# Score products in visits of three chunks, with a three-deep PSUM ring shared with the gate sums

## The chip, the cores and the metric

The kernel runs on one core of one Trainium2 chip. The metric is the device time of an execution in microseconds, given as the median of several executions. The span in a profile is mostly about 1.8 us shorter than the time of the same execution, since it starts and ends with the first and last recorded instruction.

## The reference

Softmax attention over 8 batches and 12 heads, then a gated feed-forward layer on the 3584 tokens:

```python
# q, k, v: (8, 12, 448, 64); w_gate, w_val: (768, 1536); w_out: (1536, 768)
scores = np.matmul(q, k.transpose(0, 1, 3, 2)) / np.sqrt(64)
attn = np.exp(scores - scores.max(-1, keepdims=True))
attn = attn / (attn.sum(-1, keepdims=True) + 1e-09)
x = np.matmul(attn, v).transpose(0, 2, 1, 3).reshape(3584, 768)
g = x @ w_gate
out = (g * (1 / (1 + np.exp(-g))) * (x @ w_val)) @ w_out
```

## The kernel before

Two heads make a pair, so there are 48 pairs, six to a batch. Scores are computed transposed, in four chunks of 112 key rows per pair. The contraction over 64 head dimensions uses half the array's rows, so the two heads of a pair lie in the two halves: the *64-row form*. The weighted sums and the row sums have outputs of 32 rows and use a quarter of the columns for each of four products: the *32-column form*, or quarter form. The feed-forward products use the whole array (*full form*), or are written in the quarter form where `tiled` is set, with four times as many instructions for the same work.

TensorE works in an order fixed by the program. It comes to the scores in *visits*: two chunks, then other work (a weighted sum, a row sum, gate, value and output groups), then two chunks. ScalarE turns scores into exponentials.

```python
ps_s = ctx.enter_context(tc.tile_pool(name="ps_s", bufs=2, space=PSUM))  # scores, 2 banks each
ps_a = ctx.enter_context(tc.tile_pool(name="ps_a", bufs=1, space=PSUM))  # weighted sums
ps_f = ctx.enter_context(tc.tile_pool(name="ps_f", bufs=3, space=PSUM))  # all the rest
# ...
def qk_half(pr, half, between=None):
    # ...
    for c in (2 * half, 2 * half + 1):
        s = ps_s.tile([128, 2, 512], FP32, tag="s")
        for hx in range(2):
            nc.tensor.matmul(s[:, hx, 0:S], lhsT=..., rhs=..., start=True, stop=True)
        nc.scalar.activation(E[pr][:, c], s[0:P, :, 0:S], AF.Exp, scale=sm_scale)
        # ...
def mm(dst, lhsT, rhs, start, stop):
    if not tiled[0]:
        nc.tensor.matmul(dst, lhsT=lhsT, rhs=rhs, start=start, stop=stop)
        return
    for j in range(4):
        nc.tensor.matmul(dst[ts(j, 32), :], lhsT=lhsT[:, ts(j, 32)], rhs=rhs, start=start, stop=stop)

def ffn1_steps(kk, c0, n, hts):
    for fb in range(NFB):
        gp = ps_f.tile([128, 512], FP32, tag="f")
        # six mm into gp (gate); tanh on ScalarE -> sg; yield
        vp = ps_f.tile([128, 512], FP32, tag="f")
        # six mm into vp (value); two products on VectorE -> hts; yield
```

The softmax here doesn't subtract the row's maximum and nothing guards it: scores larger than these inputs give would overflow.

## Time and profile before

| | before |
|---|---|
| time, median of 3 runs | 463.16 us (462.67 to 463.72) |
| span of the profiled execution | 460.2 us |
| TensorE busy | 452.3 us, 98% |
| ScalarE, VectorE busy | 53%, 51% |
| first score of pair 6 (the mixed stage starts) | 28.64 us |
| end of the last matmul | 456.60 us |

TensorE is the bound, and its busy share cannot show what the change is after, since a change of the array's form counts as busy time. It is read from start-to-start times in the timeline of TensorE, and from the list of waits. There "PEld" (the weight load) waiting on "issue" is a stall with no releaser. The lines themselves stand in the prediction below.

### The profile page before, as it was taken

The numbers are of one execution on the slowest core, as the hardware profiler recorded it, in microseconds if no ns is written. First come the engines' busy times: TensorE is split into PE (matmuls) and PEld (weight loads), VectorE is DVE, ScalarE is ACT, GpSimd is POOL, SyncE is SP. The second block draws the span as 40 slices with busy tenths as digits, with TensorE's granted clock in tenths as the row PEclk, the third lists the DMA queues.
The fourth block names the chain that finished last, engine by engine and source line by source line (L and its number), as shares of the span: only waits on it lengthen the run. The fifth ranks groups of instructions, "written<-read, shape, count | busy, mean of one in ns | idle before, by whom it ended". The sixth has DMA issues, their size and how long they took to land.

```text
span 460.2 us, 14133 instructions
## 1 busy us (share of the span) xinstructions
PE 452.3 (98%) x6367; PEld 227.8 (49%) x6367; DVE 236.8 (51%) x371; ACT 243.0 (53%) x353; POOL 104.2 (23%) x164
## 2 busy tenths in 40 slices
PE   8899999999999999999999999999999999999996
PEld 3344444444455555444455555544445556554454
DVE  2765663666764554564654554636555546334310
ACT  7986666656664555454646555455555562222222
POOL 8455606334150132303123040210200000000000
PEclk9999999999999999999999999999999999999999
DMA  9999999995793484662758393903603111100123
GB/s 133 195 200 201 192 180 183 223 154 80 90 113 57 78 126 49 114 102 31 118 58 119 67 131 74 142 6 76 98 10 56 37 37 36 36 11 25 36 68 103
DMA packets 82045, 44.23 MB, mean 96 GB/s; under 512 B 36673, under 2 KB 78529, under 8 KB 81985
## 3 DMA queue, kind: packets, MB, share of 16 engines
q0 software_dynamic: 42368, 23.37, 39.2%
q1 hardware_dynamic: 39520, 19.92, 23.8%
q8 instruction: 49, 0.80, 0.7%
q14 instruction: 12, 0.09, 0.1%
q10 hardware_dynamic: 96, 0.05, 0.0%
HBM read 47.19 MB, written 11.01 MB: 126 GB/s over the span
## 4 chain that ended last, share of the span: by engine, by line
PE 95%; ACT 3%; DMA 1%; DVE 0%; issue 0%; SPq 0%; ACTq 0%
PE gp L264 15%; PE op L261 14%; PE vp L264 13%; PE vp L261 11%; PE op L264 10%; PE s L196 10%; PE gp L261 9%; PE acc L212 9%; PE acc L234 4%; ACT E L203 2%; DMA rk<-in_k_dram 1%; PE tp L184 1%; PE wp L103 0%; PE tp L167 0%; DVE qkT L175 0%
## 5 line engine op out<-in xcount | busy, mean ns | idle before, releaser
L203 ACT ACTIVATE E<-s 112x896 f16<-112x896 f32 x192 | 164.6, 917 | 24.3 <-PE s L196 24.1
L280 ACT ACTIVATE sg<-gp 128x384 f32<-128x384 f32 (+1 forms) x96 | 52.3, 545 | 85.4 <-PE gp L264 54.7
L292 DVE SCALAR_TENSOR_TENSOR t<-sg,gp 128x384 f32<-128x384 f32 (+1 forms) x96 | 58.5, 610 | 64.3 <-ACT sg L280 64.2
L325 ACT ACTIVATE osb<-op 128x384 f32<-128x384 f32 (+1 forms) x57 | 27.7, 486 | 100.5 <-PE op L261 56.3
L264 PE MATMUL gp<-X,wg 128*32 128x512 f16 (+1 forms) x1416 | 78.1, 355 | 0.0
L249 DVE RECIPROCAL R<-ssb 128x112 f32<-128x112 f32 x92 | 73.1, 827 | 0.7
L295 DVE SCALAR_TENSOR_TENSOR hts<-t,vp 128x384 f16<-128x384 f32 (+1 forms) x96 | 59.6, 621 | 23.3 <-PE vp L264 7.9
L261 PE MATMUL op<-wo,hts 128*128 128x384 f16 (+1 forms) x408 | 68.6, 322 | 0.0
L264 PE MATMUL vp<-X,wv 128*32 128x512 f16 (+1 forms) x1224 | 66.9, 353 | 0.0
L226 DVE TENSOR_TENSOR X<-acc,R 128x448 f16<-128x448 f32 x48 | 29.7, 624 | 64.9 <-PE acc L212 63.1
L261 PE MATMUL vp<-X,wv 128*128 128x384 f16 (+1 forms) x270 | 58.4, 352 | 0.0
L196 PE MATMUL s<-qkT 64*128 64x448 f16 x384 | 54.8, 355 | 2.5 <-ACT E L203 2.2
L261 PEld LDWEIGHTS <-hts 128*128 128x128 f16 x408 | 38.9, 98 | 28.2 <-issue 3.0
L264 PEld LDWEIGHTS <-wg 128*32 128x32 f16 x1416 | 37.8, 97 | 29.6
L264 PE MATMUL op<-wo,hts 128*32 128x384 f16 x1104 | 48.9, 326 | 0.0
L261 PE MATMUL gp<-X,wg 128*128 128x384 f16 (+1 forms) x222 | 47.4, 350 | 0.0
L264 PEld LDWEIGHTS <-wv 128*32 128x32 f16 x1224 | 32.7, 97 | 25.5
L212 PE MATMUL acc<-E,vt 112*32 112x448 f16 x768 | 45.2, 355 | 0.0
L126 POOL DMA_DIRECT2D vt<-in_v_dram x16 | 12.3, 772 | 142.7 <-PE acc L212 141.7
L261 PEld LDWEIGHTS <-wv 128*128 128x128 f16 x270 | 25.3, 98 | 26.9 <-issue 4.8
L264 PEld LDWEIGHTS <-hts 128*32 128x32 f16 x1104 | 29.5, 97 | 16.3
L154 POOL COPY qk<-q 112x512 f16<-112x512 f16 x37 | 22.9, 620 | 63.9 <-DMA qkT<-qk 46.4
(38 smaller groups left out, 201.2 us busy)
## 6 DMA issues: line engine op xcount, KB each, us to landing
vt<-in_v_dram POOLq DMA_DIRECT2D x16, 336.0 KB, 5.2
q<-in_q_dram POOLq DMA_DIRECT2D x22, 224.0 KB, 5.9
k<-in_k_dram POOLq DMA_DIRECT2D x22, 224.0 KB, 6.7
out_dram<-osb SPq DMA_DIRECT2D x7, 336.0 KB, 3.1
wg<-in_moe_w_gate_dram POOLq DMA_DIRECT2D x8, 288.0 KB, 11.1
wv<-in_moe_w_val_dram POOLq DMA_DIRECT2D x8, 288.0 KB, 11.4
wo<-in_moe_w_out_dram POOLq DMA_DIRECT2D x2, 1152.0 KB, 21.6
out_dram<-osb SPq DMA_DIRECT2D x8, 288.0 KB, 2.9
```

Of the source, the lines that this page charges most:

```text
L154: nc.gpsimd.tensor_copy(dst, src)
L196: nc.tensor.matmul(s[:, hx, 0:S], lhsT=t[ts(hx, 64)].rearrange("p c q -> p (c q)")[:, c * P : c * P + 128], rhs=t[ts(hx, 64), NC:, :].rear ...
L203: nc.scalar.activation(E[pr][:, c], s[0:P, :, 0:S], AF.Exp, scale=sm_scale)
L212: nc.tensor.matmul(acc[ts(j, 32), 0:S], lhsT=v16[g][:, 2 * r + j % 2, c, :].rearrange("p (d t) -> p t d", t=2)[:, t], rhs=E[p0 + j // 2][: ...
L226: nc.vector.tensor_tensor(X[kk][:, hp + t, ts(bb, S)], acc[:, 0:S], R[p0][:], ALU.mult)
L249: lambda i=i: nc.vector.reciprocal(rt[:, ts(i, P)], ssb[:, ts(i, P)]) for i in range(4)
L261: nc.tensor.matmul(dst, lhsT=lhsT, rhs=rhs, start=start, stop=stop)
L264: nc.tensor.matmul(dst[ts(j, 32), :], lhsT=lhsT[:, ts(j, 32)], rhs=rhs, start=start, stop=stop)
L280: nc.scalar.activation(sg[:, 0:n], gp[:, 0:n], AF.Tanh, scale=0.5)
L292: nc.vector.scalar_tensor_tensor(t1[:, 0:n], sg[:, 0:n], 1.0, gp[:, 0:n], ALU.add, ALU.mult)
L295: nc.vector.scalar_tensor_tensor(hts[:, fb, 0:n], t1[:, 0:n], 0.5 * HS, vp[:, 0:n], ALU.mult, ALU.mult)
L325: nc.scalar.activation(osb[:, ds(m0, w)], op[:, 0:w], AF.Copy, scale=1.0 / HS)
```

## The change

The change makes the visits longer and so fewer: from pair 20 on, three chunks per visit in place of two. For this the score tiles become a ring of three (six of the eight PSUM banks), which the gate sums share. Value sums, weighted sums, row sums and outputs are left with two banks. The order of all the work is planned anew to fit.

```diff
+WIDE = 20
 ...
-    ps_s = ctx.enter_context(tc.tile_pool(name="ps_s", bufs=2, space=PSUM))
-    ps_a = ctx.enter_context(tc.tile_pool(name="ps_a", bufs=1, space=PSUM))
-    ps_f = ctx.enter_context(tc.tile_pool(name="ps_f", bufs=3, space=PSUM))
+    ps_s = ctx.enter_context(tc.tile_pool(name="ps_s", bufs=3, space=PSUM))
+    ps_f = ctx.enter_context(tc.tile_pool(name="ps_f", bufs=2, space=PSUM))
 ... (the first transposes take ps_s tiles, pv() takes ps_f tiles)
-            gp = ps_f.tile([128, 512], FP32, tag="f")
+            gp = ps_s.tile([128, 2, 512], FP32, tag="s", name="gp")[:, 0]
 ... (the loop over pairs with its backlog of groups is replaced)
+        while g < last or queue:
+            n = 2 if g < WIDE * NC else 3
+            todo = []
+            while queue and queue[0][0] <= g and len(todo) < 2:
+                todo.append(queue.pop(0))
+            plan.append(([divmod(x, NC) for x in range(g, min(g + n, last))], todo))
+            g += n
 ...
+        for x, (chunks, todo) in enumerate(plan):
 ...
+            for pr, c in chunks:
+                qk(pr, c)
 ... (one product, then gate-value pairs, the second product, output groups)
```

More of the change, by code (lines that the diff above doesn't have):

```diff
@@ L178, in turn @@
         def turn():
-            tp = ps_f.tile([128, 2 * NC, 128], FP16, tag="f", name="tp")
+            if pr < FIRST + 2:
+                tp = ps_s.tile([128, 2 * NC, 256], FP16, tag="s", name="tp")
+            else:
+                tp = ps_f.tile([128, 2 * NC, 128], FP16, tag="f", name="tp")
             for t in range(2):
@@ L187, in prep, with qk, qk_half, pv @@
         return turn if pr else turn0
-    def qk_half(pr, half, between=None):
-        if half == 0:
+    def qk(pr, c):
+        if c == 0:
             E[pr] = ep.tile([P, NC, 2, S], FP16, tag="E", name="E")
         t = qkT[pr]
-        for c in (2 * half, 2 * half + 1):
-            s = ps_s.tile([128, 2, 512], FP32, tag="s")
-            for hx in range(2):
-                nc.tensor.matmul(
-                    s[:, hx, 0:S],
-                    lhsT=t[ts(hx, 64)].rearrange("p c q -> p (c q)")[:, c * P : c * P + 128],
-                    rhs=t[ts(hx, 64), NC:, :].rearrange("p c q -> p (c q)"),
-                    start=True,
-                    stop=True,
-                )
-            nc.scalar.activation(E[pr][:, c], s[0:P, :, 0:S], AF.Exp, scale=sm_scale)
+        s = ps_s.tile([128, 2, 512], FP32, tag="s")
+        for hx in range(2):
+            nc.tensor.matmul(
+                s[:, hx, 0:S],
+                lhsT=t[ts(hx, 64)].rearrange("p c q -> p (c q)")[:, c * P : c * P + 128],
+                rhs=t[ts(hx, 64), NC:, :].rearrange("p c q -> p (c q)"),
+                start=True,
+                stop=True,
+            )
+        nc.scalar.activation(E[pr][:, c], s[0:P, :, 0:S], AF.Exp, scale=sm_scale)
+    def qk_half(pr, half, between=None):
+        for c in (2 * half, 2 * half + 1):
+            qk(pr, c)
             if between and c % 2 == 0:
                 between()
-    def pv(p0, t, pool=None):
-        acc = (pool or ps_a).tile([128, 512], FP32, tag="f" if pool else "acc", name="acc")
+    def pv(p0, t):
+        acc = ps_f.tile([128, 512], FP32, tag="f", name="acc")
         for c in range(NC):
@@ L228, in scaled, with sums @@
         )
-    def sums(p0):
-        acc = ps_f.tile([128, 512], FP32, tag="f")
+    def sums(p0, wide=False):
+        if wide:
+            acc = ps_s.tile([128, 2, 512], FP32, tag="s", name="acc")[:, 0]
+        else:
+            acc = ps_f.tile([128, 512], FP32, tag="f", name="acc")
         for c in range(NC):
@@ L385 @@
         deferred = []
-        backlog = []
-        state = {"left": 0.0}
         ffn2_wait = []
@@ L393, in pop_deferred, with add_block @@
                     deferred.pop(0)()
-        def add_block(i):
+        fvq = []
+        oq = []
+        count = {}
+        def add_block(i, visits):
             f1, f2, n = block(i)
-            t1, t2 = NCB * n / 2400.0, NFB * OH / 2400.0
-            a = [(f1, t1)] * (2 * NFB)
-            pend = list(ffn2_wait)
+            oq.extend(ffn2_wait)
             ffn2_wait.clear()
-            seq = []
-            m = len(pend)
-            done = 0
-            for x in range(len(a)):
-                seq.append(a[x])
-                want = (x + 1) * m // len(a)
-                while done < want:
-                    seq.append(pend[done])
-                    done += 1
-            seq += pend[done:]
-            own = [(f2, t2)] * (2 * (n // 128))
-            if i == 0:
-                seq += own
-            else:
-                ffn2_wait.extend(own)
-            backlog.extend(seq)
-            state["left"] += sum(t for _, t in seq)
@@ L419, in ffn_run @@
-        def ffn_run(budget):
-            while backlog and budget > 0:
-                gen, t = backlog.pop(0)
-                next(gen)
-                budget -= t
-                state["left"] -= t
-                pop_deferred(1 if t < 1.5 else 2)
-            return budget
-        carry = 0.0
-        DELAY = 2
-        END = NPAIR + 2
-        add_at = {FIRST: 0}
-        for i in range(1, B - 1):
-            add_at[NHP * (i + 1) + DELAY] = i
-        for pr in range(END):
-            slots = 2 * (min([x for x in add_at if x > pr] + [END + 0.5]) - pr)
+            fvq.extend([(f1, NCB * n / 2400.0)] * NFB)
@@ new lines, in add_block, with run_fv, run_o @@
+            own = [(f2, NFB * OH / 2400.0)] * (2 * (n // 128))
+            (oq if i == 0 else ffn2_wait).extend(own)
+            count.update(visits=visits, fv=NFB, o=len(oq), at=0, more=NFB - visits)
+        def run_fv():
+            gen, t = fvq.pop(0)
+            for _ in range(2):
+                next(gen)
+                pop_deferred()
+            return 2 * t
+        def run_o():
+            gen, t = oq.pop(0)
+            next(gen)
+            pop_deferred(2)
+            return t
@@ L436, with run_budget, left, share @@
+        def run_budget(budget):
+            while (fvq or oq) and budget > 0:
+                budget -= run_fv() if fvq else run_o()
+            return budget
+        def left():
+            return sum(2 * t for _, t in fvq) + sum(t for _, t in oq)
+        def share(total, at, n):
+            return (at + 1) * total // n - at * total // n
+        for pr in range(FIRST):
             odd = pr % 2 == 1
             turn2 = None
-            if pr == FIRST:
-                recip_act(pr - 2, sums(pr - 2))
-                load_table("exp_and_others")
-                halves = [pv(pr - 2, 0), pv(pr - 2, 1, ps_f)]
@@ L442 @@
-            if pr < NPAIR:
-                qk_half(pr, 0, prep(2) if pr == 1 else None)
+            qk_half(pr, 0, prep(2) if pr == 1 else None)
             if pr == 0:
@@ L447 @@
                 dummy(1)
-            if pr + 3 < NPAIR and pr + 3 >= NPE:
-                prep(pr + 3)
-            if not odd and 14 <= pr + LA < NPAIR:
-                load_qk16(pr + LA)
-            if pr + 2 < NPAIR:
-                if 0 < pr < NPE - 2:
-                    turn2 = prep(pr + 2)
-                if (pr + 2) % GP == GP - 1 and 4 <= (pr + 2) // GP + 1 < NGRP:
-                    load_v((pr + 2) // GP + 1)
-            if pr == FIRST:
-                for t in range(2):
-                    scaled(pr - 2, t, halves[t])
-                add_block(0)
-                ffn_run(2.5)
-            elif not odd and pr >= 2:
+            if pr > 0:
+                turn2 = prep(pr + 2)
+            if (pr + 2) % GP == GP - 1 and 4 <= (pr + 2) // GP + 1 < NGRP:
+                load_v((pr + 2) // GP + 1)
+            if pr in (2, 4):
                 deferred.extend(recips(pr - 2, sums(pr - 2)))
-                if pr < FIRST:
-                    pop_deferred(1)
+                pop_deferred(1)
             elif pr in (3, 5):
-                halves.append(pv(pr - 3, 1, ps_f))
+                halves.append(pv(pr - 3, 1))
                 pop_deferred(4)
@@ L470 @@
                     scaled(pr - 3, t, halves[t])
-            work = odd and pr > FIRST + 1
-            if work:
-                pop_deferred(4)
-                scaled(pr - 3, 0, pv(pr - 3, 0))
-            if pr in add_at and pr != FIRST:
-                add_block(add_at[pr])
             for w in wq.pop(pr, []):
                 emit(w)
-            tiled[0] = pr >= TILED
-            if pr != FIRST:
-                carry = ffn_run(state["left"] / slots + carry)
-            else:
-                slots -= 1
-            tiled[0] = False
-            if pr < NPAIR:
-                early = 1 <= pr < FIRST
-                qk_half(pr, 1, turn2 if early else None)
+            qk_half(pr, 1, turn2)
             if pr == 0:
                 dummy(2)
-            if turn2 and not early:
-                turn2()
             if pr in (2, 4):
@@ L494 @@
                 halves = [pv(pr - 2, 0)]
-            if work:
-                scaled(pr - 3, 1, pv(pr - 3, 1))
-            tiled[0] = pr >= TILED and work
-            carry = ffn_run(state["left"] / max(1, slots - 1) + carry)
+        p4 = FIRST - 2
+        recip_act(p4, sums(p4, True))
+        load_table("exp_and_others")
+        halves = [pv(p4, t) for t in range(2)]
+        queue = []
+        for p0 in range(FIRST, NPAIR, 2):
+            for kind, m in (("sums", 8), (0, 11), (1, 14)):
+                queue.append((NC * p0 + m, kind, p0))
@@ new lines @@
+        plan = []
+        g = FIRST * NC
+        last = NPAIR * NC
+        while g < last or queue:
[5 more added lines that the diff above has]
+            g += n
+        adds = {0: 0}
+        for x, (_, todo) in enumerate(plan):
+            for _, kind, p0 in todo:
+                if kind == 1 and p0 % NHP == NHP - 2 and p0 // NHP < B - 1:
+                    adds[x] = p0 // NHP
@@ new lines, in product @@
+        def product(kind, p0):
+            if kind == "sums":
+                pop_deferred(99)
+                deferred.extend(recips(p0, sums(p0)))
+            else:
+                pop_deferred(99)
+                scaled(p0, kind, pv(p0, kind))
+        carry = 0.0
+        for x, (chunks, todo) in enumerate(plan):
+            wide = not chunks or len(chunks) != 2
+            for pr, c in chunks:
+                qk(pr, c)
+            end = min([y for y in adds if y > x] + [len(plan) + 1])
+            if x == 0:
+                for t in range(2):
+                    scaled(p4, t, halves[t])
+                add_block(0, end)
+            turn2 = None
+            entered = [pr for pr, c in chunks if c == 0]
+            for pr in entered:
+                if NPE <= pr + 3 < NPAIR:
+                    prep(pr + 3)
+                if pr % 2 == 0 and 14 <= pr + LA < NPAIR:
+                    load_qk16(pr + LA)
+                if (pr + 2) % GP == GP - 1 and 4 <= (pr + 2) // GP + 1 < NGRP:
+                    load_v((pr + 2) // GP + 1)
+            for pr, c in chunks:
+                if c == 2 and pr < NPE - 2:
+                    prep(pr + 2)()
+            if todo:
+                product(*todo[0][1:])
+            if x in adds and x > 0:
+                add_block(adds[x], end - x)
+            for pr in entered:
+                for w in wq.pop(pr, []):
+                    emit(w)
+            tiled[0] = bool(todo) and (not chunks or chunks[0][0] >= TILED)
+            if adds[max(y for y in adds if y <= x)] < 2:
+                for item in todo[1:]:
+                    product(*item[1:])
+                carry = run_budget(left() / (end - x) + carry)
+            else:
+                at, n = count["at"], count["visits"]
+                no = share(count["o"], at, n)
+                nf = 1
+                if no and count["more"] > 0:
+                    o_left = sum(1 for y in range(at, n) if share(count["o"], y, n))
+                    extra = -(-count["more"] // o_left)
+                    nf += extra
+                    count["more"] -= extra
+                count["at"] += 1
+                for y in range(nf):
+                    if fvq:
+                        run_fv()
+                for item in todo[1:]:
+                    product(*item[1:])
+                for _ in range(no):
+                    run_o()
@@ L499 @@
             tiled[0] = False
-        ffn_run(1e9)
+        run_budget(1e9)
         pop_deferred(99)
-        add_block(B - 1)
-        ffn_run(1e9)
-        backlog.extend(ffn2_wait)
-        ffn_run(1e9)
+        add_block(B - 1, 1)
+        run_budget(1e9)
+        oq.extend(ffn2_wait)
+        run_budget(1e9)
 _INS = ['q', 'k', 'v', 'moe_w_gate', 'moe_w_val', 'moe_w_out']
```

## The prediction

> **What bounds the kernel now.** I read the page first: engine shares, the slices, the chain that ended last. Then the list of waits, and then the timeline of TensorE in single visits of the steady stage, with ScalarE beside it.
>
> ```profile
> PE 452.3 (98%) x6367; PEld 227.8 (49%) x6367; DVE 236.8 (51%) x371; ACT 243.0 (53%) x353; POOL 104.2 (23%) x164
> PE 95%; ACT 3%; DMA 1%; DVE 0%; issue 0%; SPq 0%; ACTq 0%
> ```
>
> TensorE is busy in 98% of the span and carries 95% of the chain that ended last; no other engine is above 53%. The 3% of ScalarE lie in the first 27 us, where only exponentials and scores exist. So only what TensorE itself does, or a wait put in front of it, can move the end. A busy share hides the cost that this change is after, though. It shows in the list of waits and in start-to-start times:
>
> ```profile
> PEld L196 <- issue: 35.2, 96, 0.7
> PEld L212 <- issue: 15.6, 44, 0.4
> PEld L261 <- issue: 11.8, 32, 0.4
> PEld L234 <- issue: 8.9, 25, 0.7
> PE s L196 <- ACT E L203: 2.2, 5, 0.4
> ```
>
> The weight loads of the scores (L196) stand still 96 times, once per visit to the scores, with no releaser: nothing is late, the array is being changed over. The weights cannot be loaded ahead there. What these stalls cost the matmuls is less than their 0.37 us each, because earlier matmuls still run. That is read from the starts (columns: start, duration, engine, line, operation):
>
> ```profile
> 253.68 1.15 PE L264 MATMUL gp<-X,wg 128*32 128x384 f16 x24
> 254.76 0.55 PE L196 MATMUL s<-qkT 64*128 64x448 f16 x4
> 255.24 0.94 PE L234 MATMUL acc<-E,ones 112*32 112x448 f16 x16
> 256.00 2.12 PE L264 MATMUL op<-wo,hts 128*32 128x384 f16 x48
> 257.96 1.15 PE L264 MATMUL vp<-X,wv 128*32 128x384 f16 x24
> 259.04 0.55 PE L196 MATMUL s<-qkT 64*128 64x448 f16 x4
> 259.52 1.15 PE L261 MATMUL gp<-X,wg 128*128 128x384 f16 x6
> 260.51 1.14 PE L261 MATMUL vp<-X,wv 128*128 128x384 f16 x6
> ```
>
> A gate or value group of 384 columns takes 0.98 us to the next start where another full-height group follows (median over the span), and 1.08 where scores follow (253.68 to 254.76, 257.96 to 259.04); with 512 columns 1.30 and 1.40. So entering the scores costs **0.10 us**. The four score matmuls take 0.48 us to the next start; in the early stage visits of two matmuls take 0.29. The second chunk therefore adds 0.19, and leaving the scores costs 0.29 - 0.19 = **0.10 us**. Between 128-column and 32-column form there is another 0.10 (0.87 against 0.77 for a weighted sum that full-width groups follow). In steady running both forms cost the same, 0.98 us for 6 full or 24 quarter matmuls, so writing more of the groups in the quarter form is neutral.
>
> **What the Trainium skill says.** The page "TensorEngine Tiling (Array Packing)", section "Key Properties", says that changing the tiling mode drains TensorE, while changing the tile does not. The trace agrees: 0.10 us at each change between 64-row, 32-column and full form, none inside one form. It gives no figure; the 0.10 is the trace's. The page "TensorE: Matmul & The Clock Gate", section "Back-to-back issue gap", has N/2.4 + 2.5 ns for a warm matmul: 162.5 ns for 384 columns, 0.975 us for six, and the trace's 0.98 agrees, so no slack is left inside a group. The page "PSUM — Partial Sum Buffer", section "PSUM bank collisions raise a hardware error", asks that an engine's access to a bank be ordered against the others' by semaphores: a ring slot is only reusable after its reader is done. The trace shows that wait five times, scores waiting on the exponential.
>
> **The change part by part.** From the instruction order of both kernels I counted stretches of one array form.
>
> *Switches.* Pairs 20 to 47 have 28 x 4 = 112 chunks: 56 visits of two before, 37 of three and one of a single chunk after, so 18 visits fewer. Entering scores falls from 99 to 81 times and leaving them likewise; changes between 32-column and full form fall from 12 to 10. All changes: 217 before, 179 after, 38 fewer, by 0.10 us = **-3.8 us**. A visit of three should take 0.48 + 0.19 = 0.67 us.
>
> *Columns streamed.* Unchanged; 288 full matmuls become four times as many quarters (864 more instructions), neutral by the above: 0.
>
> *Scores' ring and the exponential.* After a wide visit comes a 4-column product (0.77 us), then a gate group. In a ring of three, the visit's scores take all three slots and the gate group takes the slot of the first chunk, which must have been exponentiated. It wants to start 0.67 + 0.77 = 1.44 us after the visit's first score. When is that slot free? Columns again start and duration:
>
> ```profile
> 250.59 0.49 ACT L325 ACTIVATE osb<-op 128x384 f32<-128x384 f32 x1 [2.43 <-PE op L264]
> 250.98 1.72 ACT L203 ACTIVATE E<-s 112x896 f16<-112x896 f32 x2
> 252.93 0.49 ACT L280 ACTIVATE sg<-gp 128x384 f32<-128x384 f32 x1 [0.23 <-PE gp L264]
> ```
>
> The scores of this visit started at 250.47, right after an output group. ScalarE first copies that output out (0.12 after the first score), then starts the exponential at 0.51; with its mean of 0.917 us it ends at 1.43, and in the early stage a waiting score matmul started 0.05 us after the exponential's end. So the slot is free at 1.48 against 1.44 wanted: 0.02 to 0.04 us late. The new order has 31 wide visits directly after an output group: about **+0.9 us**. Visits after other work start their exponential at 0.40 and are in time (1.36).
>
> *Block starts.* The new order puts the first gate group of a block straight after the last weighted sum that fills its input; before, two pairs lay between. The scaling on VectorE ended 1.67 us after that sum's start (0.995 to begin, 0.624, 0.05); the sixth matmul step of a 384-column group wants it at 0.77 + 5 x 0.163 = 1.58, of a 512-column group at 1.85. Three narrow blocks lose about 0.09: **+0.25 us**.
>
> *Two banks for the rest.* Value sums, weighted sums, row sums and outputs now alternate in two banks. By the durations of the rows, in a visit with one gate-value pair the exponentials end 3.15 us in, tanh 3.64, the two VectorE products 4.8; the value bank is wanted again only in the next visit, after 6.1. That holds with two pairs as well. One place fails: where a block of 384 columns starts and a row sum is drawn into the same visit, all four reciprocals (0.75 each) stand before the next scaling, which ends 9.15 us in, while the second value group wants that bank at 8.8, and the output group after it waits again: about **+0.6 us**, once.
>
> *First six pairs.* Here ScalarE bounds; it was idle about 0.75 us between its first and last exponential there. The third score buffer should take away some, and the transposes, which now share the ring, give part of it back: **-0.3 us**.
>
> Sum: -3.8 + 0.9 + 0.25 + 0.6 - 0.3 = -2.35, so 463.16 - 2.35 = **460.8 us**.
>
> **The rivals.** First, that the switches are all there is: the waits of 0.02 to 0.09 us vanish, since in the profile before no TensorE wait exists between 29 and 381 us. Then 463.16 - 4.1 = 459.1. Second, that the ring becomes the bound: a margin of -0.04 us is no margin, and each further 0.1 us on the exponential (three in a row keep ScalarE and its queue behind for 3.15 us of a visit of 5.5 to 8.7) costs 31 x 0.1 = 3.1 us; with 0.15 the time is 465. For it: gate groups wait on an engine that serves in order. Against: ScalarE is only about half busy in this stage (108 of 200 us), and the order seems cut to fit. Third, that the gate sums in the ring delay the next visit's third score: its slot is free after tanh and the first product, by 4.3 us for one pair and about 7 for two, while it is wanted past 5.8 and 7.8; I expect no wait. Fourth, that a switch saved gives less than 0.10, since the first matmul after a switch is a little longer anyway; at 0.09 it is 0.4 us less.
>
> **Range and chances.** The gain cannot exceed about 4.8 us (all switches and all the early idle time), 458.4. Downward the unknown is the ring: 0.1 us more per visit ends near 463.9. I give 458.6 to 463.2. Two per cent are 9.3 us: no term reaches that for the better, and for the worse it would take a wait of 0.4 us in each wide visit. Faster 0.01, within 2% 0.97, slower 0.02.
>
> **What would show it right or wrong.** Right: scores' weight loads stalling on issue some 78 times in place of 96; six score matmuls in 0.67 us to the next start; 0.98 to 1.08 us groups as before; a short wait of the gate group on the exponential in most wide visits, together about 1 us; TensorE otherwise without waits after 29 us. Wrong: waits of the gate, value or output groups summing above 3 us, a third score that waits on VectorE, a visit of three that takes longer than 0.7 us, or an early stage that ends more than 1 us off its 28.6.

## The result and the profile after

The changed kernel takes **460.93 us** (median of 4 runs, 459.70 to 462.18). The kernel before takes 463.24 in the same rounds. The ratio is **0.9949**, 95% interval 0.9926 to 0.9972. The predicted 460.8 us is met.

The engine shares, the chain that ended last, and the instruction queue, from the page of the changed kernel:

```profile
PE 449.9 (98%) x7231; PEld 244.6 (53%) x7231; DVE 239.2 (52%) x371; ACT 240.3 (52%) x353; POOL 104.0 (23%) x164
...
q8 instruction: 56, 0.92, 0.9%
...
PE 93%; DVE 3%; ACT 2%; DMA 1%; issue 0%; DVEq 0%; ACTq 0%
```

TensorE still bounds the kernel, with 2.4 us less busy time. It has 864 more matmuls (7231 against 6367), since more groups are in the quarter form. The queue that fetches instructions moved 56 packets, 0.92 MB, where it had moved 49 and 0.80 MB. I gave that line no thought before the run, and it matters below.

The list of waits of the changed kernel (engine, line, what it waited for; us in total, times, longest):

```profile
PEld L198 <- issue: 28.9, 80, 0.8
PEld L218 <- issue: 15.3, 43, 0.4
PEld L243 <- issue: 7.4, 21, 0.4
...
PE s L198 <- ACT E L205: 1.5, 4, 0.4
```

L198 is now the scores' matmul. Its weight loads stall 80 times where it was 96: the visits are fewer, and 80 is near the predicted 78. TensorE's matmuls have no listed wait after 29 us. One wide visit of the changed kernel, TensorE and ScalarE from the timeline (start, duration, engine, line, operation):

```profile
251.25 0.74 PE L198 MATMUL s<-qkT 64*128 64x448 f16 x6
251.37 0.49 ACT L334 ACTIVATE osb<-op 128x384 f32<-128x384 f32 x1 [2.43 <-PE op L273]
251.75 2.52 ACT L205 ACTIVATE E<-s 112x896 f16<-112x896 f32 x3
251.93 0.94 PE L218 MATMUL acc<-E,vt 112*32 112x448 f16 x16
...
252.72 1.16 PE L273 MATMUL gp<-X,wg 128*32 128x384 f16 x24
...
253.69 1.16 PE L273 MATMUL vp<-X,wv 128*32 128x384 f16 x24
```

Six score matmuls take 0.68 us to the next start here (251.25 to 251.93), 0.67 over the median of the 37 wide visits. The weighted sum takes 0.79 to the gate group (251.93 to 252.72), where 0.77 would be without a wait. The profile does not list a loss of 0.02 us; only start-to-start times show it. Before the exponentials (251.75) ScalarE copies out the output group (251.37), as the prediction had it. With the mean of 0.92 us the first exponential ends at 252.67, and the gate group starts at 252.72.

Three other places cost time, all where a block of tokens ends or starts:

```profile
240.71 0.95 PE L243 MATMUL acc<-E,ones 112*32 112x448 f16 x16
241.76 2.13 PE L273 MATMUL op<-wo,hts 128*32 128x384 f16 x48
...
345.61 1.23 PE L273 MATMUL gp<-X,wg 128*32 128x384 f16 x24
346.66 1.16 PE L273 MATMUL vp<-X,wv 128*32 128x384 f16 x24
...
351.90 1.15 PE L273 MATMUL gp<-X,wg 128*32 128x384 f16 x24
353.14 1.16 PE L273 MATMUL vp<-X,wv 128*32 128x384 f16 x24
354.26 2.13 PE L273 MATMUL op<-wo,hts 128*32 128x384 f16 x48
```

A gate group followed by a value group of the same form takes 0.98. At 345.61 it takes 1.05, since its sixth step waits for the freshly scaled input (0.07 lost). At 351.90 it takes 1.24: the value bank is late by 0.26, and the output group after it by 0.14 more (353.14 to 354.26 is 1.12). At 240.71 a row sum takes 1.05 in place of 0.77: the output group behind it is 0.28 late. It starts at 241.76, and VectorE's product that it needs ends at 241.70 (start 241.15, duration 0.55).

From the first score of pair 6 to the end of the last matmul the kernel before takes 427.96 us (28.64 to 456.60) and the changed one 425.86 (28.44 to 454.30): 2.10 less. This stretch, called **the mixed stage** below, leaves the start out, which varies from execution to execution.

### The profile page after: what moved, and what is told of

It is laid out like the page before. It is cut to its first block, busy times and chain, and to the rows that moved or that the text cites. A ratio compares the mean times of both kernels' runs of the same rounds, so it can differ in the third digit from the quotient of the medians.

```text
span 457.9 us, 15867 instructions
## 1 busy us (share of the span) xinstructions
PE 449.9 (98%) x7231; PEld 244.6 (53%) x7231; DVE 239.2 (52%) x371; ACT 240.3 (52%) x353; POOL 104.0 (23%) x164
## 4 chain that ended last, share of the span: by engine, by line
PE 93%; DVE 3%; ACT 2%; DMA 1%; issue 0%; DVEq 0%; ACTq 0%
PE gp L273 16%; PE vp L273 16%; PE op L273 15%; PE op L270 9%; PE s L198 9%; PE acc L218 8%; PE gp L270 8%; PE vp L270 7%; PE acc L243 4%; ACT E L205 2%; DVE R L258 1%; DMA rq<-in_q_dram 1%; PE tp L187 1%; DVE X L232 0%; DVE ssb L255 0%
## 5 line engine op out<-in xcount | busy, mean ns | idle before, releaser
L273 PE MATMUL gp<-X,wg 128*32 128x384 f16 (+1 forms) x1608 | 87.9, 352 | 0.0
L273 PE MATMUL vp<-X,wv 128*32 128x384 f16 (+1 forms) x1608 | 87.8, 351 | 0.1
L273 PE MATMUL op<-wo,hts 128*32 128x384 f16 x1680 | 74.7, 326 | 0.1
L273 PEld LDWEIGHTS <-wv 128*32 128x32 f16 x1608 | 46.5, 97 | 29.2 <-issue 0.3
L273 PEld LDWEIGHTS <-hts 128*32 128x32 f16 x1680 | 49.2, 97 | 20.8 <-issue 0.6
L198 PE MATMUL s<-qkT 64*128 64x448 f16 x384 | 51.4, 353 | 2.4 <-ACT E L205 1.5
L270 PE MATMUL op<-wo,hts 128*128 128x384 f16 (+1 forms) x264 | 42.2, 319 | 0.0
L270 PE MATMUL gp<-X,wg 128*128 128x512 f16 (+1 forms) x174 | 38.3, 356 | 0.0
L270 PE MATMUL vp<-X,wv 128*128 128x512 f16 (+1 forms) x174 | 38.1, 355 | 0.0
L270 PEld LDWEIGHTS <-hts 128*128 128x128 f16 x264 | 25.1, 98 | 17.0 <-issue 1.9
L255 DVE COPY ssb<-acc 128x448 f32<-128x448 f32 x23 | 14.4, 624 | 35.2 <-PE acc L243 35.2
```

The source lines that it names most:

```text
L198: nc.tensor.matmul(s[:, hx, 0:S], lhsT=t[ts(hx, 64)].rearrange("p c q -> p (c q)")[:, c * P : c * P + 128], rhs=t[ts(hx, 64), NC:, :].rear ...
```

## The experiments

All were correct unless said otherwise. "Changes" are changes of the array's form, counted from the instruction order: 217 before, 179 in the changed kernel. The kernel before took 463.50, 463.34, 463.35 and 463.23 us in the rounds of the four chips.

### e0_again: the changed kernel unedited

> The changed kernel once more, unedited, for its spread and to stand beside the next three on one chip. All theories: 460.9 us, within 459.7 to 462.2 as its first four runs; a gate group that follows a product in a wide visit starts 0.79 us after that product (0.77 where nothing waits).

Measured: 461.51 us (460.11 to 463.24), ratio 0.9967 (0.9943 to 0.9990). The spread of 3 us is wider than that of the kernel before (462.1 to 464.43 in 11 runs of those rounds, in two clusters of spans near 460.4 and 461.7). Its profile, of a slow one among its executions, shows two causes. First, the start: the warm-up matmul of the changed kernel's first profile, and then of this one:

```profile
6.38 0.39 PE L103 MATMUL wp<-warm 128*128 128x512 f16 x1
```

```profile
6.83 0.61 PE L103 MATMUL wp<-warm 128*128 128x512 f16 x1
```

The same instruction takes 0.61 us in place of 0.39. TensorE ran slower here until about 10 us, and pair 6 started at 29.91 in place of 28.44: 1.5 us lost before the change has any part in it. The Trainium skill, page "TensorE: Matmul & The Clock Gate", section "Part 1: The HAM clock gate", says that the array starts at half clock and that the window which decides on the full clock runs freely, so that the same kernel has more or fewer slow matmuls from run to run. The traces agree: their record of the full clock begins at 4.71 us in the first profile and at 10.16 in this one. Second, in the middle of an output group:

```profile
178.56 0.68 PE L273 MATMUL op<-wo,hts 128*32 128x384 f16 x12
180.42 1.65 PE L273 MATMUL op<-wo,hts 128*32 128x384 f16 x36 [1.19 <-issue]
```

After 12 of 48 matmuls TensorE stands for 1.19 us, on "issue", with every operand long there. A value group at 288 us lost 0.41 in the same way. By start-to-start times 1.37 and 0.59 us are lost in the two, and 0.1 in a third place (252.5) without a listed wait; with the late start this is the whole difference of the spans (461.5 against 457.9). The trace's instruction fetches come in packets of 16 KB; one that started at 175.29 took 3.68 us where 0.97 is typical. It landed at 178.97, and TensorE went on 1.46 us later. So a **late instruction fetch** was the suspect. No fetch was held up on purpose, but a count over all traces, told below under what was right and wrong, bears it out.

### e1_two: visits of two to the end, with the new rings and the new planner

```diff
-WIDE = 20
+WIDE = 48
```

> Visits of two chunks to the end (WIDE = 48), all else as changed: the ring of three, two banks for the rest, the new order. Changes of array form rise from 179 to 215. My theory (each change costs 0.10 us, and that is the gain): +3.6 us, less about 0.6 us because in visits of two the gate group gets a slot whose reader is long done, less up to 0.7 us of block-start waits: 463.2 to 463.9 us, no better than the kernel before. Rival (the third score buffer and the new order make the gain, not the visits): stays at 460.9.

215 changes. Measured: 462.25 us (461.95 to 463.39), ratio 0.9986. In the profiles the mixed stage is 428.33 against 425.86, **2.47 us longer**, inside what I expected for the step from two to three chunks (3.6 less 0.6 less up to 0.7). It is also no shorter than that of the kernel before (427.96): the third buffer and the new order alone gain nothing, so the rival falls. The time itself is below the expected 463.2. The medians differ by only 0.7 (against e0_again) to 1.3 (against the first four runs), and the intervals of e1_two (0.9968 to 1.0004) and e0_again overlap, so the times alone do not decide. The profile of this kernel has no stall on issue within a group, and its runs spread 1.4 us, while those of the changed kernel spread 2.5 and 3.1.

### e7_tinyfull and e8_tinyhalf: the price of one change of form

In each wide visit, a matmul of 8 columns stands before the second and the third chunk (74 in all). In e7 it is in full form, which adds two changes of form each, 148 together. In e8 it is in the scores' own 64-row form and adds none. The chunk that follows overwrites its result.

```diff
+        if tiny:   # e8: warm[0:64, ...] in both operands
+            nc.tensor.matmul(s[:, 0, 0:8], lhsT=warm[:, 0:128], rhs=warm[:, 0:8], start=True, stop=True)
```

> The cost of a change of array form by itself: in each of the 37 wide visits a tiny matmul of 8 columns in full form (into the bank that the following scores overwrite; results stay right) is put before the second and before the third chunk, so 74 tiny matmuls and 148 changes of form more. My theory (0.10 us at each change): 14.8 us and at most 2 us for the tiny ones themselves, 475 to 478 us; a wide visit takes about 0.67 + 0.4 + a little = 1.1 us to the next start. Rival (a change costs less where it is not between long groups, or the saving lies in fewer instructions): under 470 us.

> The same 74 tiny matmuls of 8 columns in the 64-row form of the scores themselves: as many instructions, no change of form. My theory: 461 to 463 us, a wide visit about 0.7 us. Rival (the instructions cost it): as slow as with the full-form ones.

Measured: 474.56 us (474.55 to 475.88), ratio 1.0250, for e7, and 462.47 (460.89 to 463.48), 0.9979, for e8. The time of e7 is just under the expected 475. From its start to the next start a wide visit takes 1.108 us in e7, 0.718 in e8 and 0.671 in the changed kernel (medians of 37). The four changes of a visit thus cost 0.39 us, **0.097 us each**; over the 37 visits 14.4 us. The mixed stages, 440.61 and 427.63, agree: from that of e8 one issue stall is to be taken off, 1.08 by start-to-start times, which leaves 14.1 us between them. The small matmuls of e8 add 1.7 us to the visits, but the gate groups then no longer wait for the exponential (0.77 us after the product, not 0.79), so the mixed stage without the stall is only 0.7 longer than the changed kernel's. The lists of waits of e7, then e8:

```profile
PEld L200 <- issue: 28.8, 80, 0.7
PEld L198 <- issue: 14.8, 74, 0.2
```

```profile
PEld L200 <- issue: 29.0, 80, 0.8
```

The tiny loads (L198) stall 74 times in e7 and not at all in e8; the scores (L200) as before. Ordering alone, or the number of instructions, does not do it; the form does.

### e17_half: 64-column halves in place of 32-column quarters

```diff
-        for j in range(4):   # ts(j, 32)
+        for j in range(2):   # ts(j, 64)
```

> The groups in quarter form (four column tiles of 32) written in half form instead (two of 64 columns); all else as changed. 7231 matmuls become 4783, as many columns streamed. If a product of 32-column tiles followed by 64-column tiles counts as a change of form: some 50 changes more, 5 us more, about 466, a product to gate group at 0.87 to 0.89 us. If it does not, and late instruction fetches are what spreads the times of the changed kernel: no wait on issue inside a group, a spread of 1.4 us or less (the slow and fast start alone), and 460.0 to 460.5 us.

The same work with 4783 matmuls in place of 7231. Measured: 465.48 us (465.13 to 466.31), ratio 1.0052. The hope for a faster kernel fell. The list of waits has a new line, and the timeline shows what it costs:

```profile
PEld L273 <- issue: 19.1, 52, 0.4
```

```profile
255.92 0.94 PE L218 MATMUL acc<-E,vt 112*32 112x448 f16 x16
256.79 1.17 PE L273 MATMUL gp<-X,wg 128*64 128x384 f16 x12
```

From a 32-column product to a 64-column group it takes 0.87 us, not 0.77 to 0.79: going from 32 to 64 columns is itself a change of form. The mixed stage is 431.0, 5.14 more than 425.86, and 52 times 0.10 is 5.2. The Trainium skill, page "TensorEngine Tiling (Array Packing)", section "Available Configurations", lists 128x64 and 128x32 as separate configurations; together with the drain on a change of mode, that is what this run shows. I had missed it. On the other side, this kernel's profile has no stall on issue within a group, and its six runs lie within 1.2 us, which fits the late fetches.

### e13_tiled6: the quarter form from the start of the mixed stage

```diff
-TILED = 14
+TILED = 6
```

> Quarter form for the groups that follow a product from pair 6 on instead of from pair 14 (TILED = 6): changes of form fall from 179 to 170, 360 matmuls more. My prediction's step (the quarter form is neutral): 0.9 us less, 460.0 to 460.6. New theory (the quarter form quadruples the instructions that TensorE has to fetch, and where transfers are dense a late fetch stops it for about 1 us in some executions): as many or more waits on issue of a group in its middle, a wider spread of the times, and no gain: 461 to 463.

170 changes. Measured: 460.73 us (460.26 to 462.36, 6 runs), ratio 0.9949, just above the expected 460.6. The mixed stage is 425.36. One stall on issue of 0.27 at 193 us is in it (0.44 by start-to-start times), so without it 424.9: 0.96 less than 425.86, and 9 changes by 0.10 are 0.9. So the quarter form is neutral in steady running, as predicted. It also speaks against my idea that fetches come late where transfers are dense: the first 83 us are the densest of the kernel, the quarter form was put there, and no group stalled there.

### e9_late: copying an output group out after the next visit's first exponential

```diff
+                if hold[0]:
+                    yield 0.0
                 nc.scalar.activation(osb[:, ds(m0, w)], op[:, 0:w], AF.Copy, scale=1.0 / HS)
```

Where the next visit has three chunks, the copy is held back and issued after the first chunk's exponential.

> In the wide stage the copy of an output group out of its bank is put on ScalarE's queue behind the first exponential of the next visit instead of ahead of it. My theory (the gate group waits 0.02 us in each of some 31 visits because that copy delays the exponential from 0.40 to 0.51): product to gate group falls from 0.79 to 0.77 us and the time by 0.6 us, to about 460.3. Rival (the 0.02 us is the changeover or the weight load, not the exponential): 0.79 and 460.9 stay.

Measured: 460.38 us (459.33 to 462.1), ratio 0.9934 (0.9914 to 0.9953). From the product to the gate group it takes 0.77 where it was 0.79, so the wait on the ring is gone. In the changed kernel 31 gate groups were 0.022 to 0.033 late, 0.79 us in all; here none is. Also, the scores that follow an output group came 2.070 us after its start in the changed kernel and come 2.056 after it here, as in the kernel before (0.36 in all); why they were late was not looked into. The mixed stage of its profile is 426.64, with two stalls on issue (1.12 and 0.2 by start-to-start times). Without them it would be 425.3, 0.5 below 425.86: a longer wait (a value group on VectorE's scaling, 0.56 where it was 0.27) and lesser ones take back part of the 1.15. Its interval overlaps that of e0_again, so by times alone the gain is unclear; the start-to-start times show it.

### e14_first: e9_late, with the visit's second product straight after the first

```diff
+            if len(chunks) == 3:
+                for item in todo[1:]:
+                    product(*item[1:])
+                todo = todo[:1]
```

> Two waits taken out of the changed kernel: the copy-out behind the first exponential of the next visit (as in the earlier run that was faster), and, where a visit has two products, both straight after the scores, so that the reciprocals start about 2 us earlier and the first gate group of a block comes 0.77 us later. My theory: product to gate group 0.77 us; the waits at the block starts (0.07 to 0.09 us three times), of an output group on the products of VectorE (0.29 us) and of a value group on the scaling (0.26 to 0.55 and 0.14 us) are gone: 1.2 us less than changed, another 0.9 us less than the copy-out alone; 459.5 to 460.2 us. Rival (late fetches hide it): no clear difference.

Measured: 460.80 us (459.46 to 461.84), ratio 0.9939, above the expected 460.2. The waits at 240.71 and 351.90 went, and so did two of the three at block starts; a new one came, four times:

```profile
181.03 0.94 PE L218 MATMUL acc<-E,vt 112*32 112x448 f16 x16
182.11 0.94 PE L243 MATMUL acc<-E,ones 112*32 112x448 f16 x16
```

The second product takes the bank of the output group whose copy is now held behind an exponential: 1.08 us between the products in place of 0.77. The two edits are in each other's way where a visit has two products. (One stall on issue, 1.18 by start-to-start times, fell in this profile too.)

### e4_wide6: visits of three from pair 6

```diff
-WIDE = 20
+WIDE = 6
```

> Visits of three from pair 6 on instead of from pair 20 (WIDE = 6). Changes of array form fall from 179 to 158. My theory: 21 x 0.10 = 2.1 us less, a little of it lost to waits on ScalarE, which is busier there: 458.5 to 459.5 us. Rival (wide visits cost as much in ring waits as they save, above all where ScalarE is busier): 460.9 or more.

158 changes, 21 fewer. Measured: 462.56 us (461.2 to 465.3), ratio 0.9991, in place of a gain of some 2 us. New waits stand in place of the saved changes:

```profile
PE op L273 <- DVE hts L304: 1.0, 4, 0.4
PE gp L270 <- DMA wv<-in_moe_w_val_dram: 0.8, 1, 0.8
PE gp L270 <- ACT E L205: 0.6, 1, 0.6
```

With the lesser ones (scores on VectorE, values still on their way) these add up to some 4.7 us by start-to-start times, of which a late fetch in a weighted sum at 302.6 has about 0.5. Wider visits pay only where the other engines and the loads have slack.

### e2_ring2: the same order with a ring of two

```diff
-    ps_s = ctx.enter_context(tc.tile_pool(name="ps_s", bufs=3, space=PSUM))
-    ps_f = ctx.enter_context(tc.tile_pool(name="ps_f", bufs=2, space=PSUM))
+    ps_s = ctx.enter_context(tc.tile_pool(name="ps_s", bufs=2, space=PSUM))
+    ps_f = ctx.enter_context(tc.tile_pool(name="ps_f", bufs=4, space=PSUM))
```

> Visits of three with the old ring of two double banks (and four single banks for the rest; the gate sums stay in the ring): what the third double bank is for. My theory: the third chunk of each of 37 visits waits for the first exponential, till about 1.47 us in place of 0.40, so 1.0 to 1.1 us each, and gate groups wait for the second one besides: 40 us or more, 500 us or more. Rival (ring depth hardly matters because ScalarE is half idle): under 470 us.

Measured: 513.39 us (2 runs), ratio 1.1086. The waits, then one visit from the timeline:

```profile
PE s L198 <- ACT E L205: 35.7, 45, 0.9
PE gp L270 <- ACT E L205: 6.1, 9, 1.5
```

```profile
252.94 0.37 PE L198 MATMUL s<-qkT 64*128 64x448 f16 x2 [0.92 <-ACT E L205]
```

The third chunk of a wide visit waits for the first exponential each time. Some 37 times 1.08 us by start-to-start times, 6.1 on gate groups, and an early stage that ends 5.3 us later (33.73 us) account for the 52 us of the span. The ring of three is what makes visits of three possible. This is the second rival of the prediction, "the ring becomes the bound", brought about on purpose.

### e18_all: the useful edits together

`TILED = 6`; the copy-out held back, except ahead of a visit with two products; both products straight after the scores.

```diff
-            hold[0] = x + 1 < len(plan) and len(plan[x + 1][0]) == 3
+            hold[0] = x + 1 < len(plan) and len(plan[x + 1][0]) == 3 and len(plan[x + 1][1]) == 1
```

> What the runs so far found, together: quarter form after a product from pair 6 on (9 changes of form fewer), copy-out behind the first exponential of the next visit except ahead of visits with two products (which made the second product wait 0.32 us four times), and both products of a visit straight after the scores. My theory: 0.9 + 0.6 + 0.9 us less than changed where no fetch is late, from the first gate group to the last matmul about 423.5 us against 425.9; 458.7 to 459.5 us as a median. Rival (what is taken from one wait comes back in the next): 460.5 or more.

Measured: **459.06 us** (458.45 to 460.15, 6 runs), ratio 0.9915 (0.9898 to 0.9932). The mixed stage is 425.32. One wait in it has nothing to do with the edits' aims:

```profile
65.45 2.13 PE L279 MATMUL op<-wo,hts 128*32 128x384 f16 x48 [1.54 <-DMA wo<-in_moe_w_out_dram]
```

The first output group waits for the output weights, which are loaded behind a value chunk that is needed much later. By start-to-start times this costs 1.72, and a stall on issue in another output group 0.44; without the two the mixed stage would be 423.2.

### e20_final: e18_all, three chunks from pair 14, output weights loaded first

```diff
-WIDE = 20
+WIDE = 14
 ...
-            6: [("V", 3), ("o", 0)],
+            6: [("o", 0), ("V", 3)],
```

> The version of e18_all with two more edits. Visits of three start at pair 14 in place of 20: 162 changes of array form in place of 170, so -0.8 us. And the first half of the output weights is loaded ahead of the value chunk of pairs 9 to 11: the profile of e18_all has one output group that waits 1.54 us for those weights at 63.9, and the values are first needed near 79. If TensorE's order and that wait are what is left, the time is 457.0 to 458.3 us against 459.06, with no wait on the output weights, and the stretch from pair 6's first score to the last matmul is 423.0 to 424.0 in place of 425.3. If the longer stretch of wide visits makes new waits as it did with visits of three from pair 6 on (scores or output groups waiting on VectorE and on value chunks), or if the value chunk then comes too late, it is 459 to 461 and the profile lists those waits. Late instruction fetches may add about 1 us to single executions under both.

Measured: **458.44 us** (458.16 to 460.76, 6 runs, four of them under 458.7), ratio 0.9912 (0.9891 to 0.9933). The same place in its timeline:

```profile
64.19 0.94 PE L218 MATMUL acc<-E,vt 112*32 112x448 f16 x16
64.97 2.13 PE L279 MATMUL op<-wo,hts 128*32 128x384 f16 x48
```

No wait is left there. The mixed stage is 423.01 us, 2.3 less than in e18_all and at the lower end of the expectation; it still has one stall on issue in a value group at 246 us (0.51, or 0.69 by start-to-start times). No new wait on VectorE or a value chunk is listed, so the rival is out. The median gained only 0.6 on e18_all and is 0.1 above the expected range, and the intervals of the two ratios overlap. One profile of each can't tell how many executions had the wait on the weights or a slow start (pair 6 started at 28.57 in the profile of e18_all and at 29.79 in this one). Of the kernels run here it is the fastest; its advantage over e18_all is unclear. Against the kernel before it is 0.9912. Against the changed kernel (0.9949, and 0.9967 when repeated) its interval lies apart from that of the repeat and overlaps that of the first rounds by 0.0007.

## Why the prediction was right or wrong

The prediction was right in the number and most steps. That it came within 0.13 us is in part luck: the changed kernel's runs spread 2.5 us, its repeat was at 461.51, and terms that were missed or mis-sized cancel in the sum. The terms against what they measured, by start-to-start times in the profiles before and after:

| step | predicted, us | measured, us | from |
|---|---|---|---|
| 38 changes fewer | -3.8 | -3.9 | 38 x 0.102 where they stand; 0.097 by e7 less e8 |
| gate group behind a full ring | +0.9 | +0.79 | 31 gate groups; gone in e9 |
| scores behind an output group | none | +0.36 | 2.070 for 2.056; gone in e9 |
| block starts | +0.25 | +0.23 | three gate groups, 0.07 to 0.09 late |
| reciprocals ahead of a scaling | +0.6 | +0.40 | 0.26 + 0.14, at 351.90 |
| row sum ahead of an output group | none | +0.28 | 240.71 |
| inside one form | 0 | -0.26 | what is left to the 2.10 of the mixed stage |
| first six pairs | -0.3 | -0.28 | pair 6 starts 0.20 earlier, the first transposes 0.08 later |
| sum | -2.35 | -2.4 | |

The first transposes took up their work 0.08 us later, so the span should differ by about -2.3; it does (460.2 to 457.9). One sum of the prediction slips: its bound of 4.8 us, "all switches and all the early idle time", is 4.55 by its own 3.8 and 0.75.

- **Switches.** Right in kind and size. e7 and e8 separate the change of form from the instruction that brings it. The fourth rival (a switch saved gives 0.09) did not come: 0.097 by e7 and e8, 0.102 where the switches stand.
- **The ring and the exponential.** The mechanism was right: the wait is in the visits after an output group, and holding the copy-out back took it away (e9). The size was nearly right too, 0.022 to 0.033 in 31 places for the predicted 0.02 to 0.04 in 31. The second rival, 0.1 more in each, did not come; e2 shows what a ring without the third buffer costs. Missed was that the scores behind an output group would start 0.014 later.
- **Two banks for the rest.** Right in place and cause, 0.40 in place of 0.6. The step "One place fails" missed a second place: at 240.71 a row sum stands between a value group and the output group that needs that group's product, where a gate group stood before. VectorE's last product is then still under way: it ends 0.06 us before the output group starts. In e14, where the products were moved ahead, the wait went.
- **The third rival**, a third score that waits on VectorE, did not come in the changed kernel. It came in e4 (0.3 us).
- **The formula from the skill.** The prediction's 0.975 us for six matmuls is an estimate from N/2.4 + 2.5 ns, which the Trainium skill, page "TensorE: Matmul & The Clock Gate", section "Back-to-back issue gap", gives for an isolated matmul; it says that at large N this counts too much in a stream. Here it did not: groups of six took 0.975 to 0.986 us to the next start with 384 columns and 1.295 to 1.306 with 512, and the measurement decides.
- **The step that failed in part** is "Columns streamed ... neutral: 0". In steady running it is true (e13), and it held in the two profiles compared. But in some executions TensorE stands still for 0.1 to 1.2 us on issue inside work in the quarter form. Profiles of e0_again, e4, e8, e9, e13, e14, e18_all and e20_final have one or two such stalls; those of the kernel before, the changed kernel's first, e1, e2, e7 and e17 have none. This would be why the median gains less than the profile of e1 promised (0.7 to 1.3 us of 2.47) and why the changed kernel's runs spread 2.5 and 3.1 us where those of e1 spread 1.4; that link is argued, since only the profiled executions can be looked into.

That the stalls are late fetches comes out of the traces. I counted TensorE's rows, matmuls and weight loads together. All nine listed stalls come after row 193 of a block of 256 rows, counted from the first row of the trace; 7 packets more for 1728 rows more (864 matmuls, each with its weight load) makes some 247 rows a packet, so a block is one packet. Then I set the landing of each packet against the moment when TensorE reached its block (the first packet of a trace belongs to the block that starts with row 450): 698 places in the 13 profiles without e2. In the nine with a stall the packet had landed less than 1.1 us before, or not yet. In all others it had landed 1.12 us before or more, and there is no stall; the four nearest lost at most some 0.2 us. TensorE went on 1.2 to 1.7 us after the landing. The closest packet was 1.4 us ahead in the changed kernel's first profile, 1.7 in e7, over 3 in the kernel before and in e1, and over 6 in e17, whose blocks last 9.6 us and more where those of the changed kernel last 5.2 and more.

What stays open: what holds a fetch up. In eight of the nine stalls the packet itself took an ordinary 0.9 to 1.4 us; it started late, 3.4 to 4.5 us after TensorE had entered the block before, where the median of the blocks in quarter form is 0.02. In e0_again both stalls lay near transposing transfers of small packets that took 2.6 and 3.0 us, but e13 put the quarter form into the densest transfers and saw nothing there. Why three of e7's four runs have nearly one time, with as many quarters, is not explained; its 14 us of added stalls may give the fetch time. And the kernel before was profiled once: that it has no late fetches is not shown.

## What to carry to other kernels

When TensorE is the bound at 98%, count how often its array changes form, price one change with a pair of tiny matmuls (one that changes the form, one that does not), and gather products of one form into longer visits as far as the PSUM ring and the engine that empties it allow. Give the ring one slot for each product of a visit, and put into each visit's order first what frees the slot that is wanted next. Before writing work in four times as many instructions, look at the line of the instruction queue and at how long before its use each packet lands, and judge by several executions: one profile may show none of the late fetches that the median pays for.

## What the Trainium skill lacked or had wrong

- Page "TensorEngine Tiling (Array Packing)": it says that a change of mode drains TensorE and gives no figure. Here one change cost 0.097 us (148 changes, 14.4 us).
- The same page does not say in "Key Properties" that a different column width alone is a change of mode, though its list of configurations has the widths apart. From 32 to 64 columns cost 0.10 us here, 52 times (5.14 us).
- Page "Runtime: NRT & Kernel Launch", section "Instruction fetch mechanics": it has the fetch in blocks of 16 KiB, as here, and calls its cost mostly hidden; the one fetch stall that it names is that of a taken branch. Here TensorE stalled nine times in profiles of work split into four column tiles, 0.1 to 1.2 us on issue, each time where the block's packet had landed less than 1.1 us before or not yet.
- Page "TensorE: Matmul & The Clock Gate": it has the run-to-run change of the slow start, as here, and a warm-up of some 3.4 us. The full clock began 3.5 us after the first matmul in one profile (1.19 to 4.71 us) and 9.0 us after it in another (1.19 to 10.16, with TensorE busy in 97% of the time from 2 to 10 us). Matmuls of 512 columns took 0.61 us in place of 0.39 until then, and pair 6 started 1.5 us later.
